# Pacing the MLP evenly over the attention units of a fused top-k attention and MLP kernel

## The chip, the cores and the metric

The kernel runs on one core of one Trainium2 chip. The metric is device time in microseconds (us): 2143.3 us is the median of three runs before the change (2143.25 to 2144.95).

The engines are named as in the profile: PE (TensorE, matrix products; PEld is its weight loads), DVE (VectorE), ACT (ScalarE), POOL (GpSimd), and SP, whose queue issues the DMAs. Each engine works through its own instructions in the order of the program and waits for the others through semaphores.

## The reference

A top-k attention is followed by a two-layer MLP, all in float32. Batch 8, 8 heads, 576 tokens, head size 64; 4608 tokens, model width 512, hidden width 2048.

```
scores = q @ k.T / sqrt(64)
kth    = 32nd largest of each row
scores = where(scores >= kth, scores, -1e9)
attn   = exp(scores - max) / (sum + 1e-9)
x      = (attn @ v), heads side by side      # (4608, 512)
h      = x @ w_in                            # (4608, 2048)
out    = max(0.01 * h, h) @ w_out            # (4608, 512)
```

The weights w_in and w_out arrive as float64. The kernel loads their two 32-bit words and rounds them to float32 itself.

## The kernel before

**Units.** Attention goes in 144 units. A unit is 128 query rows of a pair of heads (two score tiles of 128 x 576), or the 64 rows left over of two pairs of heads. Per batch there are 16 whole units and 2 left-over ones. A unit passes through `scores` (PE products of 64-row operands, then two ACT copies from PSUM to SBUF), `top_k` (four rounds on DVE: MAX8 for both tiles, and in three of them MATCH_REPLACE8, so 14 instructions over 576 elements), `mask` (POOL: for each tile a compare-and-scale into `pen`, and an addition), `exponents` (ACT, with the row sum), `reciprocals` (POOL adds 1e-9, DVE inverts), `normalize` (ACT, one per tile), `transpose_main` (four PE transposes per tile and an ACT copy), `transpose_tail` (two transposes and a copy), and `weigh_values` (PE products with v, ACT copy into the MLP's input x).

**MLP.** Tokens are cut into chunks of mostly 384 (`CHUNKS`, line 51). A chunk's `mlp` is a generator: 16 column blocks f of the hidden layer (4 products `ph` each, then a Prelu on ACT into `gT`), and then per 128 tokens 16 products `pz`, an ACT copy and an output DMA. It yields a cost in columns, so that the caller can issue it in pieces. Both of its PSUM tags together have two buffers.

**Order.** The program's order is written out by hand. Step s of the main loop (lines 340 to 382) handles four units at different ages: top-k of unit s, scores of unit s + 1, mask, exponents, reciprocals and normalize of unit s - 1, and transposes and values of unit s - 2. Five calls of `mlp_steps` lie between these parts, and each adds 1720 cost units to what MLP work may be issued, as long as a chunk is ready. A chunk is ready when the last of its units has passed `weigh_values`.

**Weights.** There are 32 weight chunks of 512 KB. `convert` (twice per step) converts up to two chunks and fetches up to two. `convert_weights` (lines 96 to 113) takes DVE, POOL, ACT, DVE and POOL in turn for one chunk: two integer operations on DVE (lines 104 and 105), a clamp on POOL, two ACT conversions, two more DVE operations (lines 109 and 111) and POOL's product (line 113).

**Loads.** SP's queue issues all loads and stores in program order. q, k and v of a pair of heads are 0.29 MB each, and six of each may be held (`LOADED`). At the start six pairs' q, k and v and two weight chunks are issued before any conversion.

Of the kernel before, what the change touches and what calls it, by code (L numbers as in the profile page):

```python
# [18 lines left out]
def kernel(  # L19
# [28 lines left out]
    KMAX = KLEN[-1]  # L48
    LEFT = S % P
    assert D == 64 and S == 576 and HP == 4 and B % 2 == 0 and LEFT == 64  # L50
    CHUNKS = [256] + [384] * 10 + [256, 128, 128]
    assert sum(CHUNKS) == B * S
    CHMAX = max(CHUNKS)
    LOADED = 6
# [1 line left out]
    const = ctx.enter_context(tc.tile_pool(name="const", bufs=1))  # L56
    xpool = ctx.enter_context(tc.tile_pool(name="xpool", bufs=2))
    loads = ctx.enter_context(tc.tile_pool(name="loads", bufs=LOADED))
    raws = ctx.enter_context(tc.tile_pool(name="raws", bufs=2))
    work = ctx.enter_context(tc.tile_pool(name="work", bufs=2))  # L60
    small = ctx.enter_context(tc.tile_pool(name="small", bufs=4))
    ps_sc = ctx.enter_context(tc.tile_pool(name="ps_sc", bufs=1, space=bass.MemoryType.PSUM))
    ps_tr = ctx.enter_context(tc.tile_pool(name="ps_tr", bufs=2, space=bass.MemoryType.PSUM))
    ps_ml = ctx.enter_context(tc.tile_pool(name="ps_ml", bufs=2, space=bass.MemoryType.PSUM))
# [31 lines left out]
    def convert_weights(dst, raw):  # L96

        lo, hi = raw[:, :, 0], raw[:, :, 1]  # L100
        ex = raws.tile([P, WCH], U32, name="ex")
        man = raws.tile([P, WCH], U32, name="man")
        frac = raws.tile([P, WCH], F32, name="frac")
        nc.vector.tensor_scalar(ex, hi, 20, 0x7FF, ALU.logical_shift_right, ALU.bitwise_and)
        nc.vector.tensor_scalar(man, hi, 0xFFFFF, None, ALU.bitwise_and)
        nc.gpsimd.tensor_scalar(ex, ex, 1151.0, 896.0, ALU.min, ALU.max)  # L106
        nc.scalar.activation(frac, lo, AF.Copy, bias=1.0, scale=2.0 ** -52)
        nc.scalar.activation(ex, ex, AF.Copy, bias=-896.0 * 2.0 ** 23, scale=2.0 ** 23)  # L108
        nc.vector.scalar_tensor_tensor(out=frac, in0=man, scalar=2.0 ** -20, in1=frac,
                                       op0=ALU.mult, op1=ALU.add)  # L110
        nc.vector.scalar_tensor_tensor(out=ex, in0=hi, scalar=0x80000000, in1=ex,  # L111
                                       op0=ALU.bitwise_and, op1=ALU.bitwise_or)
        nc.gpsimd.tensor_tensor(dst, frac, ex.bitcast(F32), ALU.mult)
# [42 lines left out]
    def scores(u):  # L156
        ps = [ps_sc.tile([P, 2, 512], F32, name=f"psc{i}") for i in range(2)]
        for n in range(0, len(u.parts), 2):
            for half in range(2):
                for i, pi, side, r0 in u.parts[n:n + 2]:  # L160
                    qt, kt = qk_of[pi]
                    d = slice(side * D, (side + 1) * D)
                    nc.tensor.matmul(  # L163
                        ps[i][r0:r0 + u.rows, half, 0:HS],
                        qt[d, u.q0:u.q0 + u.rows],
                        kt[d, half * HS:(half + 1) * HS],
                        start=True, stop=True,
                    )
        u.s = []
        for i in range(2):  # L170
            s_sb = work.tile([P, S], F32, name=f"s_sb{i}", bufs=4)
            nc.scalar.copy(s_sb.rearrange("p (h n) -> p h n", h=2), ps[i][:, :, 0:HS])  # L172
            u.s.append(s_sb)

# [12 lines left out]
                src = rest  # L187
            yield

    def mask(u):  # L190
        u.nbias = small.tile([P, 2], F32, name="nbias")
        u.z = small.tile([P, 2], F32, name="z")
        nc.gpsimd.tensor_scalar(u.nbias, u.tops[:, :, 0, 0], -SCALE, None, ALU.mult)
        for i in range(2):
            pen = work.tile([P, S], F32, name="pen")
            nc.gpsimd.tensor_scalar(pen, u.s[i], u.tops[:, i, ROUNDS - 1, 7:8], MASKED,  # L196
                                    ALU.is_lt, ALU.mult)
            nc.gpsimd.tensor_tensor(u.s[i], u.s[i], pen, ALU.add)  # L198

    def exponents(u, i):  # L200
        nc.scalar.activation(u.s[i], u.s[i], AF.Exp, bias=u.nbias[:, i:i + 1], scale=SCALE,  # L201
                             accum_out=u.z[:, i:i + 1])

    def reciprocals(u):
        ze = small.tile([P, 2], F32, name="ze")
        u.rz = small.tile([P, 2], F32, name="rz")
        nc.gpsimd.tensor_scalar(ze, u.z, 1e-9, None, ALU.add)  # L207
        nc.vector.reciprocal(u.rz, ze)  # L208

    def normalize(u, i):  # L210
        nc.scalar.activation(u.s[i], u.s[i], AF.Copy, bias=0.0, scale=u.rz[:, i:i + 1])  # L211
# [48 lines left out]
    def mlp(ch):  # L260

        n = CHUNKS[ch]
        t0 = sum(CHUNKS[:ch])
        x = x_of[ch]
        for f in range(NFC):
            ph = ps_ml.tile([P, 512], F32, name="ph", tag="ml")
            for c in range(HP):
                nc.tensor.matmul(  # L268
                    ph[:, 0:n], w_in[c][:, f * P:(f + 1) * P], x[c][:, 0:n],
                    start=(c == 0), stop=(c == HP - 1),  # L270
                )
            nc.scalar.activation(gT[f][:, 0:n], ph[:, 0:n], AF.Prelu, alpha=SLOPE)  # L272
            yield 4 * max(n, 225)
        for i in range(n // P):
            pz = ps_ml.tile([P, 512], F32, name="pz", tag="ml")
            for f in range(NFC):
                nc.tensor.matmul(  # L277
                    pz[:, 0:DMODEL], gT[f][:, i * P:(i + 1) * P], w_out[f // 4][:, f % 4, :],
                    start=(f == 0), stop=(f == NFC - 1),
                )  # L280
                if f % 4 == 3 and f + 1 < NFC:
                    yield 4 * DMODEL
            o_sb = work.tile([P, DMODEL], F32, name="o_sb")
            nc.scalar.copy(o_sb, pz[:, 0:DMODEL])
            nc.sync.dma_start(out[t0 + i * P:t0 + (i + 1) * P, :], o_sb)
            yield 4 * DMODEL

    ready, owed, running = [], [0.0], [None]
    BUDGET = 1720

    def mlp_steps(budget=BUDGET):
        owed[0] += budget
        while owed[0] > 0:
            if running[0] is None:
                if not ready:
                    owed[0] = 0.0
                    return
                running[0] = mlp(ready.pop(0))
            cost = next(running[0], None)
            if cost is None:  # L300
                running[0] = None
            else:
                owed[0] -= cost

    def unit(n):
        return units[n] if 0 <= n < len(units) else None

    done_tokens = [0] * len(CHUNKS)  # L310

    def attended(u):
        ch, _ = x_at(u.b * S + u.q0)
        done_tokens[ch] += u.rows * len(u.pairs)
        if done_tokens[ch] == CHUNKS[ch] * HP:
            ready.append(ch)

    chunks, raw_chunks = weight_chunks(), []

    def fetch_weights():  # L320
        chunk = next(chunks, None)
        got = load_weights(*chunk) if chunk else None
        if got:
            raw_chunks.append(got)

    with tc.manual_schedule():
        last = {p: n for n, u in enumerate(units) for p in u.pairs}
        load_qk(0)
        scores(units[0])
        for _ in range(2):  # L330
            fetch_weights()

        def load_more(s):

            for of, load, lag in ((qk_of, load_qk, -1), (v_of, load_v, 2)):
                while len(of) < NPAIR and (len(of) < LOADED or last[len(of) - LOADED] + lag <= s):
                    load(len(of))

        load_more(-1)
        for s in range(len(units) + 3):  # L340
            cur, new, old, older = unit(s), unit(s + 1), unit(s - 1), unit(s - 2)
            picks = top_k(cur) if cur else iter(())

            def convert():
                for _ in range(2):
                    if raw_chunks:
                        convert_weights(*raw_chunks.pop(0))
                    fetch_weights()

            if old:  # L350
                mask(old)
            next(picks, None)
            if new:
                scores(new)
            convert()
            mlp_steps()
            next(picks, None)
            if older:
                transpose_main(older, 0)
            mlp_steps()  # L360
            if older:
                transpose_main(older, 1)
            convert()
            mlp_steps()
            next(picks, None)
            if older:
                transpose_tail(older)
            if old:
                exponents(old, 0)
            mlp_steps()  # L370
            if old:
                exponents(old, 1)
                reciprocals(old)
            if older:
                weigh_values(older)
                attended(older)
            mlp_steps()
            next(picks, None)
            if old:
                normalize(old, 0)  # L380
                normalize(old, 1)
            load_more(s)
        mlp_steps(1e9)


# [43 lines left out]
```

## Time and profile before

| what | value |
|---|---|
| median of three runs | 2143.3 us (2143.25 to 2144.95) |
| the profiled execution | 2140.65 us |
| its span, first to last instruction | 2138.9 us |
| mean granted TensorE clock | 0.920 |
| PE busy | 1743.4 us (82%) |
| DVE busy | 1496.2 us (70%) |
| POOL busy | 1174.4 us (55%) |
| ACT busy | 975.9 us (46%) |

Busy times are shares of the span. A stretch (window) of the trace gives the same figures for a part of the span, with the granted clock as a fraction of full speed. A timeline lists instructions in order of time, with equal neighbours merged. A line of the waits says which engine's instruction stood idle for which engine's result, with the sum, the number and the longest.

### The profile page before, as it was taken

The numbers are of one execution on the slowest core, as the hardware profiler recorded it, in microseconds if no ns is written. First come the engines' busy times: TensorE is split into PE (matmuls) and PEld (weight loads), VectorE is DVE, ScalarE is ACT, GpSimd is POOL, SyncE is SP. The second block draws the span as 40 slices with busy tenths as digits, with TensorE's granted clock in tenths as the row PEclk, the third lists the DMA queues.
The fourth block names the chain that finished last, engine by engine and source line by source line (L and its number), as shares of the span: only waits on it lengthen the run. The fifth ranks groups of instructions, "written<-read, shape, count | busy, mean of one in ns | idle before, by whom it ended". The sixth has DMA issues, their size and how long they took to land.

```text
span 2138.9 us, 25069 instructions
## 1 busy us (share of the span) xinstructions
PE 1743.4 (82%) x8864; PEld 1065.6 (50%) x8864; DVE 1496.2 (70%) x3152; ACT 975.9 (46%) x2069; POOL 1174.4 (55%) x934
## 2 busy tenths in 40 slices
PE   1122796897897898898898898798798799699898
PEld 1111554554554554554554554554554555454665
DVE  4788859758857857857857856956955955955760
ACT  1333545435435534535544544544544543543442
POOL 3666547546646645645645645745744844744551
PEclk9999997998898899898799799799799699799999
DMA  4222001000100001000100001000100001000000
GB/s 158 79 79 86 13 10 60 8 9 18 40 22 11 0 6 59 19 6 11 46 21 16 1 6 55 23 1 15 45 17 21 1 1 38 12 1 15 1 10 11
DMA packets 22973, 56.20 MB, mean 26 GB/s; under 512 B 2240, under 2 KB 2240, under 8 KB 22848
## 3 DMA queue, kind: packets, MB, share of 16 engines
q1 hardware_dynamic: 22848, 54.60, 7.5%
q8 instruction: 70, 1.15, 0.2%
q14 instruction: 55, 0.45, 0.1%
HBM read 45.15 MB, written 9.44 MB: 26 GB/s over the span
## 4 chain that ended last, share of the span: by engine, by line
PE 59%; DVE 27%; POOL 7%; ACT 4%; issue 1%; DMA 1%; SPq 0%; POOLq 0%; ACTq 0%; DVEq 0%
PE ph L268 23%; PE pz L277 23%; DVE tops L182 14%; DVE rest L185 12%; PE psc L163 4%; PE main L218 4%; PE po L248 4%; POOL pen L196 3%; POOL s_sb L198 2%; ACT s_sb L201 1%; DVE ex L111 1%; POOL ex L106 1%; ACT ex L108 1%; DMA raw<-in_moe_w_in_dram 1%; PE tail L225 1%
## 5 line engine op out<-in xcount | busy, mean ns | idle before, releaser
L196 POOL TENSOR_SCALAR pen<-s_sb,tops 128x576 f32<-128x576 f32 x288 | 641.3, 2227 | 109.3 <-DVE tops L182 108.7
L182 DVE MAX8 tops<-rest 128x8 f32<-128x576 f32 x864 | 607.9, 745 | 0.0
L268 PE MATMUL ph<-x,w_in 128*128 128x384 f32 (+2 forms) x1792 | 543.7, 451 | 7.5 <-ACT x L258 7.5
L277 PE MATMUL pz<-w_out,gT 128*128 128x512 f32 x1152 | 524.6, 599 | 0.0
L185 DVE MATCH_REPLACE8 rest<-tops,rest 128x576 f32<-128x576 f32 x576 | 423.3, 743 | 0.0
L198 POOL TENSOR_TENSOR s_sb<-s_sb,pen 128x576 f32<-128x576 f32 x288 | 405.8, 1409 | 24.0
L207 POOL TENSOR_SCALAR ze<-z 128x2 f32<-128x2 f32 x144 | 32.4, 225 | 692.1 <-ACT s_sb L201 687.6
L208 DVE RECIPROCAL rz<-ze 128x2 f32<-128x2 f32 x144 | 23.1, 160 | 548.3 <-POOL ze L207 548.3
L268 PEld LDWEIGHTS ph<-x,w_in 128*128 128x128 f32 x1792 | 312.4, 193 | 174.6 <-issue 25.2
L218 PE MATMUL main<-ident,s_sb 128*115 128x128 f32 x1152 | 218.6, 334 | 213.5 <-ACT s_sb L211 213.5
L218 PEld LDWEIGHTS main<-ident,s_sb 128*115 128x115 f32 x1152 | 190.8, 224 | 304.4 <-ACT s_sb L211 226.3
L277 PEld LDWEIGHTS pz<-w_out,gT 128*128 128x128 f32 x1152 | 207.6, 190 | 227.8 <-issue 227.2
L201 ACT ACTIVATE s_sb<-s_sb,nbias 128x576 f32<-128x576 f32 x288 | 222.8, 777 | 207.8 <-POOL s_sb L198 207.8
L248 PE MATMUL po<-wT,vt 115*64 115x128 f32 (+3 forms) x3200 | 250.1, 320 | 43.9 <-ACT wT L226 36.7
L248 PEld LDWEIGHTS po<-wT,vt 115*64 115x64 f32 (+1 forms) x3200 | 208.0, 173 | 104.9 <-ACT wT L226 39.1
L272 ACT ACTIVATE gT<-ph 128x384 f32<-128x384 f32 (+2 forms) x224 | 99.8, 445 | 332.7 <-PE ph L268 332.7
L163 PE MATMUL psc<-kt,qt 64*128 64x288 f32 (+1 forms) x1280 | 222.7, 474 | 34.4 <-ACT s_sb L172 27.0
L211 ACT ACTIVATE s_sb<-s_sb,rz 128x576 f32<-128x576 f32 x288 | 207.2, 768 | 53.6 <-DVE rz L208 53.6
L172 ACT COPY s_sb<-psc 128x576 f32<-128x576 f32 x288 | 167.7, 633 | 108.9 <-PE psc L163 108.9
L185 DVE MATCH_REPLACE8 rest<-tops,s_sb 128x576 f32<-128x576 f32 x288 | 211.7, 743 | 0.0
L220 ACT COPY wT<-main 115x512 f32<-115x512 f32 x288 | 163.1, 590 | 99.6 <-PE main L218 99.0
L182 DVE MAX8 tops<-s_sb 128x8 f32<-128x576 f32 x288 | 201.9, 743 | 7.5 <-ACT s_sb L172 7.5
(26 smaller groups left out, 703.4 us busy)
## 6 DMA issues: line engine op xcount, KB each, us to landing
vt<-in_vk_dram SPq DMA_DIRECT2D x32, 290.0 KB
qt<-in_qT_dram SPq DMA_DIRECT2D x32, 288.0 KB
kt<-in_kT_dram SPq DMA_DIRECT2D x32, 288.0 KB
out_dram<-o_sb SPq DMA_DIRECT2D x36, 256.0 KB
raw<-in_moe_w_in_dram SPq DMA_DIRECT2D x16, 512.0 KB
raw<-in_moe_w_out_dram SPq DMA_DIRECT2D x16, 512.0 KB
```

The source lines that it names most:

```text
L163: nc.tensor.matmul(ps[i][r0:r0 + u.rows, half, 0:HS], qt[d, u.q0:u.q0 + u.rows], kt[d, half * HS:(half + 1) * HS], start=True, stop=True,)
L172: nc.scalar.copy(s_sb.rearrange("p (h n) -> p h n", h=2), ps[i][:, :, 0:HS])
L182: nc.vector.max(out=u.tops[:, i, r, :], in_=src[i])
L185: nc.vector.match_replace(out=rest[i], in_to_replace=u.tops[:, i, r, :], in_values=src[i], imm_value=LOWEST)
L196: nc.gpsimd.tensor_scalar(pen, u.s[i], u.tops[:, i, ROUNDS - 1, 7:8], MASKED, ALU.is_lt, ALU.mult)
L198: nc.gpsimd.tensor_tensor(u.s[i], u.s[i], pen, ALU.add)
L201: nc.scalar.activation(u.s[i], u.s[i], AF.Exp, bias=u.nbias[:, i:i + 1], scale=SCALE, accum_out=u.z[:, i:i + 1])
L211: nc.scalar.activation(u.s[i], u.s[i], AF.Copy, bias=0.0, scale=u.rz[:, i:i + 1])
L218: nc.tensor.transpose(main[0:KLEN[c], c, :], u.s[i][:, c * KSTEP:c * KSTEP + KLEN[c]], ident)
L248: nc.tensor.matmul(po[side * D:(side + 1) * D, o, :], vt[0:KLEN[c], c, side, :], u.wT[0:KLEN[c], i, c, r0:r0 + n], start=(c == 0), stop=(c ...
L268: nc.tensor.matmul(ph[:, 0:n], w_in[c][:, f * P:(f + 1) * P], x[c][:, 0:n], start=(c == 0), stop=(c == HP - 1),)
L277: nc.tensor.matmul(pz[:, 0:DMODEL], gT[f][:, i * P:(i + 1) * P], w_out[f // 4][:, f % 4, :], start=(f == 0), stop=(f == NFC - 1),)
```

## The change

- `CHUNKS` begins with 128 and 256 tokens and ends with 256 and 128.
- `mlp` yields twice as often: in the middle of a `ph` block, and after every second `pz` product. `mlp_steps` takes its budget as an argument. `slot_budget` divides the MLP work that is ready and not yet issued by the number of slots (six per step) up to and with the step at which the next chunk gets ready.
- The softmax chain is one step longer. Mask stays with unit s - 1, but its two tiles are issued apart; exponents and reciprocals are now with unit s - 2, and normalize, transposes and values with unit s - 3 (`LAG = 3`). A chunk becomes ready at the end of the step of its last unit. `s_sb` has five buffers for four, `small` five for four, `pen` one for two. The addition of 1e-9 is a function of its own (`sums`).
- A weight conversion has two stages. The first ends after the ACT conversions; the rest is issued by the next call of `convert`. `convert` now handles one chunk and is called three times in odd steps and four times in even ones. `raw` has three buffers for two, and `frac` lies in the raw tile itself.
- At the start four pairs' q and k alternate with four weight chunks on SP's queue, and four v loads follow. Further loads start at step 4.

```diff
-    CHUNKS = [256] + [384] * 10 + [256, 128, 128]
+    CHUNKS = [128, 256] + [384] * 10 + [256, 128]
...
+        frac = lo.bitcast(F32)
+        ex = raws.tile([P, WCH], U32, name="ex", bufs=2)
+        man = raws.tile([P, WCH], U32, name="man", bufs=2)
...
         nc.scalar.activation(ex, ex, AF.Copy, bias=-896.0 * 2.0 ** 23, scale=2.0 ** 23)
+        yield
         nc.vector.scalar_tensor_tensor(out=frac, in0=man, scalar=2.0 ** -20, in1=frac,
...
+    def mask(u, i):
+        if i == 0:
+            u.nbias = small.tile([P, 2], F32, name="nbias")
+            u.z = small.tile([P, 2], F32, name="z")
+            nc.gpsimd.tensor_scalar(u.nbias, u.tops[:, :, 0, 0], -SCALE, None, ALU.mult)
+        pen = work.tile([P, S], F32, name="pen", bufs=1)
...
+    def sums(u):
+        u.ze = small.tile([P, 2], F32, name="ze")
+        nc.gpsimd.tensor_scalar(u.ze, u.z, 1e-9, None, ALU.add)
...
+                if c == 1:
+                    yield 2 * max(n, 225)
...
-                if f % 4 == 3 and f + 1 < NFC:
-                    yield 4 * DMODEL
+                if f % 2 and f + 1 < NFC:
+                    yield 2 * DMODEL
...
+    def mlp_cost(ch):
+        n = CHUNKS[ch]
+        return NFC * HP * max(n, 225) + n // P * NFC * DMODEL
...
+    for n, u in enumerate(units):
         ch, _ = x_at(u.b * S + u.q0)
         done_tokens[ch] += u.rows * len(u.pairs)
         if done_tokens[ch] == CHUNKS[ch] * HP:
+            ready_at.append((n + LAG, ch))
...
+    def slot_budget(s):
+        after = [at for at, _ in ready_at if at >= s]
+        return backlog[0] / ((after[0] + 1 - s if after else 1) * SLOTS)
...
+    def finish_conversions():
+        while converting:
+            next(converting.pop(0), None)
+    def convert():
+        finish_conversions()
+        if raw_chunks:
+            converting.append(convert_weights(*raw_chunks.pop(0)))
+            next(converting[0])
+        fetch_weights()
...
         scores(units[0])
+        fetch_weights()
+        for p in range(1, HP):
+            load_qk(p)
+            fetch_weights()
+        for p in range(HP):
+            load_v(p)
...
+            budget = slot_budget(s)
+            next(picks, None)
+            if old:
+                mask(old, 0)
+            if new:
+                scores(new)
+            convert()
+            mlp_steps(budget)
+            if older:
+                exponents(older, 0)
+            if oldest:
+                normalize(oldest, 0)
+            if older:
+                exponents(older, 1)
+                sums(older)
+            if old:
+                mask(old, 1)
+            mlp_steps(budget)
+            next(picks, None)
+            convert()
+            if oldest:
+                transpose_main(oldest, 0)
+                normalize(oldest, 1)
+            mlp_steps(budget)
+            if oldest:
+                transpose_main(oldest, 1)
+            next(picks, None)
+            convert()
+            mlp_steps(budget)
+            if older:
+                reciprocals(older)
+            if oldest:
+                transpose_tail(oldest)
+            next(picks, None)
+            if s % 2 == 0:
+                convert()
+            mlp_steps(budget)
+            if oldest:
+                weigh_values(oldest)
+            mlp_steps(budget)
+            attended(s)
+            if s >= HP:
+                load_more(s)
```

## Rows read from the trace of the kernel before

**Rows 1.** The page: busy time of each engine, and the chain's shares.

```profile
PE 1743.4 (82%) x8864; PEld 1065.6 (50%) x8864; DVE 1496.2 (70%) x3152; ACT 975.9 (46%) x2069; POOL 1174.4 (55%) x934
...
PE 59%; DVE 27%; POOL 7%; ACT 4%; issue 1%; DMA 1%; SPq 0%; POOLq 0%; ACTq 0%; DVEq 0%
```

**Rows 2.** Windows: stretch, length, busy per engine (instructions), clock, DMA share, GB/s.

```profile
0.00:45.61 45.61, 10.23 (x32) 5.99 (x32) 20.27 (x36) 10.13 (x16) 9.00 (x15) 1.00 0.54 186
46.00:228.00 182.00, 45.49 (x229) 30.60 (x230) 149.20 (x260) 68.28 (x133) 112.40 (x99) 1.00 0.23 75
390.00:495.00 105.00, 102.68 (x431) 56.24 (x428) 62.78 (x137) 41.32 (x89) 49.03 (x38) 1.00 0.02 6
495.00:555.00 60.00, 39.85 (x260) 29.41 (x259) 55.27 (x121) 36.55 (x77) 44.29 (x35) 0.73 0.11 35
2106.83:2138.90 32.07, 28.29 (x162) 20.29 (x160) 0.00 (x0) 5.29 (x18) 0.00 (x0) 1.00 0.02 9
```

**Rows 3.** Timeline of DVE (start, duration, instruction): reciprocals of two units in succession.

```profile
509.79 0.15 DVE L208 RECIPROCAL rz<-ze 128x2 f32<-128x2 f32 x1
...
519.49 0.15 DVE L208 RECIPROCAL rz<-ze 128x2 f32<-128x2 f32 x1
```

**Rows 4.** Timeline of PE through most of a step in a PE-bound stretch.

```profile
434.28 1.24 PE L163 MATMUL psc<-kt,qt 64*128 64x288 f32 x8
435.45 2.85 PE L268 MATMUL ph<-x,w_in 128*128 128x384 f32 x8
438.13 0.60 PE L218 MATMUL main<-ident,s_sb 128*115 128x128 f32 x4
438.57 2.75 PE L268 MATMUL ph<-x,w_in 128*128 128x384 f32 x8
441.15 0.60 PE L218 MATMUL main<-ident,s_sb 128*115 128x128 f32 x4
...
444.17 0.38 PE L225 MATMUL tail<-ident,s_sb 128*116 128x128 f32 x2
444.39 3.60 PE L277 MATMUL pz<-w_out,gT 128*128 128x512 f32 x8
447.92 1.31 PE L248 MATMUL po<-wT,vt 115*64 115x128 f32 x20
```

**Rows 5.** Timeline of PE: the last chunk of 128 tokens.

```profile
2106.83 14.56 PE L268 MATMUL ph<-x,w_in 128*128 128x128 f32 x128
2121.22 13.90 PE L277 MATMUL pz<-w_out,gT 128*128 128x512 f32 x32
```

**Rows 6.** Groups of ACT: busy us, mean ns of one, idle before and its releaser.

```profile
L201 ACT ACTIVATE s_sb<-s_sb,nbias 128x576 f32<-128x576 f32 x288 | 222.8, 777 | 207.8 <-POOL s_sb L198 207.8
L211 ACT ACTIVATE s_sb<-s_sb,rz 128x576 f32<-128x576 f32 x288 | 207.2, 768 | 53.6 <-DVE rz L208 53.6
L172 ACT COPY s_sb<-psc 128x576 f32<-128x576 f32 x288 | 167.7, 633 | 108.9 <-PE psc L163 108.9
L220 ACT COPY wT<-main 115x512 f32<-115x512 f32 x288 | 163.1, 590 | 99.6 <-PE main L218 99.0
L272 ACT ACTIVATE gT<-ph 128x384 f32<-128x384 f32 x160 | 78.6, 491 | 281.2 <-PE ph L268 281.2
```

**Rows 7.** Waits: who waited for whom, us in total, times, longest.

```profile
PE main L218 <- ACT s_sb L211: 213.5, 70, 27.2
...
DVE ex L111 <- ACT ex L108: 30.3, 31, 3.8
```

**Rows 8.** Groups of DVE: the two integer operations of a weight conversion.

```profile
L105 DVE TENSOR_SCALAR man<-raw 128x512 uint32<-128x512 uint32 x32 | 30.5, 953 | 0.0
...
L104 DVE TENSOR_SCALAR ex<-raw 128x512 uint32<-128x512 uint32 x32 | 15.8, 494 | 14.3 <-DMA raw<-in_moe_w_in_dram 14.3
```

**Rows 9.** Timeline of DVE in a conversion that follows another.

```profile
133.76 1.49 DVE L105 TENSOR_SCALAR man<-raw 128x512 uint32<-128x512 uint32 x1
```

More of the change, by code (lines that the diff above doesn't have):

```diff
@@ L58 @@
     loads = ctx.enter_context(tc.tile_pool(name="loads", bufs=LOADED))
-    raws = ctx.enter_context(tc.tile_pool(name="raws", bufs=2))
+    raws = ctx.enter_context(tc.tile_pool(name="raws", bufs=3))
     work = ctx.enter_context(tc.tile_pool(name="work", bufs=2))
-    small = ctx.enter_context(tc.tile_pool(name="small", bufs=4))
+    small = ctx.enter_context(tc.tile_pool(name="small", bufs=5))
     ps_sc = ctx.enter_context(tc.tile_pool(name="ps_sc", bufs=1, space=bass.MemoryType.PSUM))
@@ L100, in convert_weights @@
         lo, hi = raw[:, :, 0], raw[:, :, 1]
-        ex = raws.tile([P, WCH], U32, name="ex")
-        man = raws.tile([P, WCH], U32, name="man")
-        frac = raws.tile([P, WCH], F32, name="frac")
+        frac = lo.bitcast(F32)
+        ex = raws.tile([P, WCH], U32, name="ex", bufs=2)
+        man = raws.tile([P, WCH], U32, name="man", bufs=2)
         nc.vector.tensor_scalar(ex, hi, 20, 0x7FF, ALU.logical_shift_right, ALU.bitwise_and)
@@ L170, in scores @@
         for i in range(2):
-            s_sb = work.tile([P, S], F32, name=f"s_sb{i}", bufs=4)
+            s_sb = work.tile([P, S], F32, name=f"s_sb{i}", bufs=5)
             nc.scalar.copy(s_sb.rearrange("p (h n) -> p h n", h=2), ps[i][:, :, 0:HS])
@@ L188, in top_k @@
             yield
[L190 to L198, printed above, removed]
+    def mask(u, i):
[4 more added lines that the diff above has]
+        pen = work.tile([P, S], F32, name="pen", bufs=1)
+        nc.gpsimd.tensor_scalar(pen, u.s[i], u.tops[:, i, ROUNDS - 1, 7:8], MASKED,
+                                ALU.is_lt, ALU.mult)
+        nc.gpsimd.tensor_tensor(u.s[i], u.s[i], pen, ALU.add)
     def exponents(u, i):
@@ L202, in exponents @@
                              accum_out=u.z[:, i:i + 1])
+    def sums(u):
+        u.ze = small.tile([P, 2], F32, name="ze")
+        nc.gpsimd.tensor_scalar(u.ze, u.z, 1e-9, None, ALU.add)
     def reciprocals(u):
-        ze = small.tile([P, 2], F32, name="ze")
         u.rz = small.tile([P, 2], F32, name="rz")
-        nc.gpsimd.tensor_scalar(ze, u.z, 1e-9, None, ALU.add)
-        nc.vector.reciprocal(u.rz, ze)
+        nc.vector.reciprocal(u.rz, u.ze)
     def normalize(u, i):
@@ L271, in mlp @@
                 )
+                if c == 1:
+                    yield 2 * max(n, 225)
             nc.scalar.activation(gT[f][:, 0:n], ph[:, 0:n], AF.Prelu, alpha=SLOPE)
-            yield 4 * max(n, 225)
+            yield 2 * max(n, 225)
         for i in range(n // P):
@@ L285, in mlp, with mlp_steps @@
             nc.sync.dma_start(out[t0 + i * P:t0 + (i + 1) * P, :], o_sb)
[L286 to L291, printed above, removed]
+            yield 2 * DMODEL
+    def mlp_cost(ch):
+        n = CHUNKS[ch]
+        return NFC * HP * max(n, 225) + n // P * NFC * DMODEL
+    ready, running = [], [None]
+    backlog, owed = [0.0], [0.0]
+    def mlp_steps(budget):
         owed[0] += budget
@@ L303, in mlp_steps @@
                 owed[0] -= cost
+                backlog[0] -= cost
+    LAG = 3
     def unit(n):
         return units[n] if 0 <= n < len(units) else None
-    done_tokens = [0] * len(CHUNKS)
-    def attended(u):
+    done_tokens, ready_at = [0] * len(CHUNKS), []
+    for n, u in enumerate(units):
         ch, _ = x_at(u.b * S + u.q0)
@@ L315, in attended @@
         if done_tokens[ch] == CHUNKS[ch] * HP:
-            ready.append(ch)
+            ready_at.append((n + LAG, ch))
+    assert [ch for _, ch in ready_at] == list(range(len(CHUNKS)))
+    def attended(s):
+        for at, ch in ready_at:
+            if at == s:
+                ready.append(ch)
+                backlog[0] += mlp_cost(ch)
+    def slot_budget(s):
+        after = [at for at, _ in ready_at if at >= s]
+        return backlog[0] / ((after[0] + 1 - s if after else 1) * SLOTS)
+    SLOTS = 6
+    converting = []
     chunks, raw_chunks = weight_chunks(), []
@@ L329 @@
         scores(units[0])
-        for _ in range(2):
+        fetch_weights()
+        for p in range(1, HP):
+            load_qk(p)
             fetch_weights()
+        for p in range(HP):
+            load_v(p)
         def load_more(s):
-            for of, load, lag in ((qk_of, load_qk, -1), (v_of, load_v, 2)):
+            for of, load, lag in ((qk_of, load_qk, -1), (v_of, load_v, LAG)):
                 while len(of) < NPAIR and (len(of) < LOADED or last[len(of) - LOADED] + lag <= s):
                     load(len(of))
-        load_more(-1)
-        for s in range(len(units) + 3):
-            cur, new, old, older = unit(s), unit(s + 1), unit(s - 1), unit(s - 2)
+        for s in range(len(units) + LAG):
+            cur, new, old = unit(s), unit(s + 1), unit(s - 1)
+            older, oldest = unit(s - 2), unit(s - LAG)
             picks = top_k(cur) if cur else iter(())
[L344 to L348, printed above, removed]
+            budget = slot_budget(s)
+            next(picks, None)
             if old:
-                mask(old)
-            next(picks, None)
+                mask(old, 0)
             if new:
@@ L355 @@
             convert()
-            mlp_steps()
-            next(picks, None)
-            if older:
[L359 to L364, printed above, removed]
-            next(picks, None)
[L366 to L382, printed above, removed]
+            mlp_steps(budget)
[9 more added lines that the diff above has]
+            mlp_steps(budget)
+            next(picks, None)
+            convert()
[8 more added lines that the diff above has]
+            mlp_steps(budget)
+            if older:
+                reciprocals(older)
+            if oldest:
+                transpose_tail(oldest)
+            next(picks, None)
+            if s % 2 == 0:
[7 more added lines that the diff above has]
+                load_more(s)
+        finish_conversions()
         mlp_steps(1e9)
```

## The prediction

> **What bounds the kernel now.** I read the page's busy shares and the chain of waits first. PE is busy 82% of the span and DVE 70%, and the chain that ended last is PE for 59% and DVE for 27% [rows 1]: no single engine bounds it, so it must be two in turn. The windows show that. From 390 to 495 us PE is busy 102.7 of 105 us at granted clock 1.00 while DVE works 62.8; from 495 to 555 DVE is busy 55.3 of 60 while PE has 39.9 at a mean clock of 0.73 [rows 2]. The two stretches are one round of 12 units, one 384-token chunk. The old budget gives 5 × 1720 = 8600 cost units per unit of attention, and a chunk costs 16·4·384 + 3·16·512 = 49,152, so its MLP is done in 5.7 units (PE-bound, 105 us) and the other 6.3 run at DVE's pace, 9.70 us from one reciprocal to the next [rows 3], 61 us. A round is 165 us, 13.75 us per unit. Ahead of the rounds lies a start in which PE does little: 0 to 46 us, with DVE busy 20 us, then seven steps of 26.0 us (46 to 228) that convert four weight chunks each [rows 2].
>
> **The change, part by part.** The sum is made against the profiled execution: span 2138.9 us, 2140.65 us in all, so 1.75 lie around the span. The median of the runs shown is 2.65 us higher; that is added at the end.
>
> *PE's own work per unit, full clock* [rows 4]. Scores 1.17 us (434.28 to 435.45), two groups of main transposes 0.44 each (438.13 to 438.57), tail 0.22, value product 1.3: 3.57. The 16 left-over units of 144 have up to twice the score and value work: 0.25 on average. MLP: one f of a 384 chunk is 2.58 us (438.57 to 441.15), 16 make 41.3; one 128-row output group is 13.8 (32 instructions in 13.9 [rows 5]), three make 41.4; 82.7 per chunk, 6.89 per unit. Together 10.7 us. The check: one chunk's 82.7 plus 5.7 units × 3.57 is 103, and the PE-bound stretch holds 102.7 [rows 2].
>
> *Even pacing.* With MLP spread over 12 units, each step has 10.7 us of PE and 9.75 of DVE (9.70 [rows 3] plus the waits around the reciprocal). Neither is idle half the round any more, so the floor is PE's 10.7.
>
> *The new order within a step, which I think decides.* In before, `normalize(old)` is the last thing in a step, so PE's transposes wait for it in the DVE-bound stretch only (213.5 us in 70 waits [rows 7]). In after, ACT's in-order queue has in each step: two score copies of the new unit, exp, normalize 0, exp, copy of main 0, normalize 1. The copies wait for PE's scores at the step's start, and normalize 1 must end before PE's main 1. From the start of the scores that is 1.24 (scores) + 2 × 0.633 + 0.777 + 0.768 + 0.777 + 0.590 + 0.768 [rows 4, 6] = 6.2, plus a Prelu of 0.49 for each f that ends in slots 1 and 2 (0.9 of them in the ph half of a chunk, none in the pz half: 0.2 on average), so 6.4. PE's own work up to that point is 1.17 + 3 slots × 1.15 + 0.44 = 5.06. PE stands about 1.3 us per step, in front of main 0 and main 1. After main 1 three slots, tail and value product follow, whose copies are done in time. So 12.0 us per unit. Bounds: 10.7 if ACT gets ahead, and 12.9 if two Prelus stand in the chain and every hand-over costs 0.1 (6.2 + 1.0 + 0.1 − 5.06 = 2.2).
>
> *The other waits added.* `sums` on POOL waits for ACT's second exp; the second mask pair stands behind it, but its exp comes a whole step later. DVE's reciprocal, now ahead of the last pick round, waits for `sums`; that round (1.4 us) and the next unit's picks stand behind it. At 12.0 us a step DVE has 2.2 us to spare, so I cost it at nothing; without the slack it would be up to 1.4 per step. `pen` in one buffer is written and read by POOL alone, in order: nothing. Half-size MLP yields add no instruction: nothing. The extra `s_sb`, `small` and `raw` buffers only remove waits.
>
> *The start.* The same 32 conversions remain. DVE is busy 149.2 us in seven steps of four [rows 2], so (149.2 − 7 × 9.75) / 28 = 2.9 us each. What two stages remove is DVE's in-line wait for ACT's exponent (30.3 us in 31 waits, up to 3.8 [rows 7]), since a round of picks now lies between. On SP, 8 score loads and 3 raw chunks, then 4 value loads, replace 12 score and 6 value loads ahead of the third raw chunk; raw 4 waits for the first conversion's second stage with the value loads behind it, which nobody needs before step 3. DVE's 25 idle us at the start [rows 2] should halve to 13. At 4, 3, 4, 3... conversions a step, 32 are done at the end of step 8: 9 × 9.75 + 32 × 2.9 + 13 + 6 for hand-overs with POOL = 200 us. Before, step 8 ends at 228 + 9.7 = 238. Gain 38, bounds 15 and 50.
>
> *A rule against this.* The second integer operation of a conversion took 1.49 us beside POOL's product [rows 9]; it is 0.95 on average and the first 0.49, with one shape [rows 8]. The Trainium skill, "SBUF — State Buffer" (Who interferes with whom), says that DVE in a two-port mode and GpSimd hold their shared ports for a whole instruction; that row agrees. By that rule, and with conversions now meeting POOL's mask between picks, each might wait a whole pen operation. The sum by it would be some 40 us later, an estimate from POOL's mean of 2.2 us. My sum keeps 2.9 per conversion, which already holds such waits.
>
> *Steps 9 to 26* run the 128 and 256 chunks at 3.5 and 4.6 us of MLP a step. DVE needs 9.75; the ACT chain gives 6.4 + 0.44 + three short slots 2.2 + 0.22 + 1.3 = 10.5. I take 11.0, as the clock may dip where PE is 75% busy (0.73 at 66% [rows 2]); bounds 10 and 12. 18 × 11.0 = 198.
>
> *Steps 27 to 134*: nine 384 chunks, 108 units × 12.0 = 1296 (1156 to 1393).
>
> *Steps 135 to 142*: the tenth chunk in 8 steps, 82.7 + 8 × 3.8 = 113; slots are long enough to cover the ACT chain. *Steps 143 to 146*: the 256 chunk, 16 × 1.73 + 2 × 13.8 = 55, and four units' transposes and values, 10: 65. (One f at 256 is two thirds of 2.58.) *Last*: the 128 chunk alone, 32.07 us as before [rows 2, 5].
>
> Sum: 200 + 198 + 1296 + 113 + 65 + 32 = 1904, with 1.75 around it 1906, and 2.65 to the median: 1908.
>
> **Rivals.** *A, PE back to back*: ACT's chain hides, 10.7 a unit, 108 × 1.3 = 140 less: 1768. For it: PE was busy 98% of a stretch with all of attention in it [rows 2]. Against: there no normalize stood behind the same step's score copies.
>
> *B, longer chain*: both Prelus in it, 12.9 a unit (+97), and longer steps at the start: 2005 to 2045. For it: ACT has some twelve short instructions a step and each hand-over is in series. Against: their mean durations already hold the queueing in before.
>
> *C, the clock, slower than before*: PE's new gaps in every step bring the granted clock down all through steps 27 to 134, and PE's work stretches. In the DVE-bound stretch PE had gaps in every unit and the clock was 0.73 [rows 2]; at that, 10.7 / 0.73 = 14.7 a unit, 108 × 2.7 = 291 more: about 2200. It decides below 0.75, where a unit costs 14.2 and the sum meets 2143. Against: that stretch had a third of the work per unit, and where PE was 98% busy the clock was 1.00; I expect 89%.
>
> **How the numbers follow.** Forecast (a unit of 11.5 to 12.5: 1850 to 1965) 0.55; A and what lies toward it 0.18; B 0.22; C 0.05. The likeliest time is 1908. The range leaves out C, the upper end of B and the lowest end of A: 1775 to 2020. Faster by over 0.2% (what the runs can tell from no change) 0.95, within 0.2% 0.01, slower 0.04.
>
> **What would show it.** Windows of 12 units anywhere from 500 to 1700 us should be alike: PE about 89% busy, DVE about 80%, clock 0.97 or more, and 144 us long. The waits should show PE's main transposes on ACT's normalize about 1.3 us per unit, in two pieces, and reciprocals 12.0 us apart. DVE's waits for ACT's exponent in the conversions should be gone and step 8 end near 200 us. I am wrong if the reciprocals stand 10.7 apart (A), if ACT's waits per unit exceed 2 us (B), or if the clock of those windows is below 0.9 (C).

## The result and the profile after

The changed kernel takes 1967.5 us, the median of four runs (1965.1 to 1969.7). Against the kernel before, timed beside it, the ratio is 0.918, with a 95% interval of 0.916 to 0.919: 176 us faster. The forecast was 1908, the range 1775 to 2020. The profiled execution has a span of 1967.9 us.

The page's busy times and its chain's shares, as in [rows 1]:

```profile
PE 1651.5 (84%) x8864; PEld 963.6 (49%) x8864; DVE 1498.1 (76%) x3152; ACT 987.9 (50%) x2069; POOL 1189.6 (60%) x934
...
PE 71%; ACT 18%; POOL 4%; issue 3%; DVE 2%; DMA 0%; SPq 0%; POOLq 0%; ACTq 0%
```

DVE has gone from the chain (27% to 2%), and ACT has come in (4% to 18%) although its own work is the same. So PE and DVE no longer take turns, and a wait between PE and ACT is the new bound.

Windows of the changed kernel (stretch, length, busy PE, PEld, DVE, ACT, POOL, then clock, DMA share, GB/s): up to step 1, the start from step 1 to step 8, the even part from step 27 to 134, and the end from where PE begins the 256-token chunk.

```profile
0.00:26.92 26.92, 7.41 (x24) 4.28 (x24) 18.32 (x34) 7.67 (x12) 7.89 (x13) 1.00 0.61 203
26.92:210.22 183.30, 52.96 (x285) 40.53 (x285) 156.09 (x280) 70.53 (x140) 129.57 (x104) 0.75 0.28 91
408.00:1748.00 1340.00, 1213.64 (x6452) 680.86 (x6452) 1057.91 (x2268) 710.40 (x1479) 833.40 (x648) 0.99 0.06 21
1871.00:1967.90 96.90, 93.16 (x472) 64.44 (x470) 2.18 (x6) 29.49 (x72) 11.78 (x10) 1.00 0.03 11
```

The even part is 108 units in 1340 us, 12.4 us a unit, with PE busy 91%, DVE 79%, and the clock at 0.99. In [rows 2] PE and DVE were each over 90% busy in turn, and the clock was 0.73 in one of the two stretches. Two reciprocals of this part, in DVE's timeline, stand 12.18 us apart; in [rows 3] it was 9.70 in a DVE-bound stretch:

```profile
539.32 0.17 DVE L211 RECIPROCAL rz<-ze 128x2 f32<-128x2 f32 x1 [2.38 <-POOL ze L207]
...
551.50 0.17 DVE L211 RECIPROCAL rz<-ze 128x2 f32<-128x2 f32 x1 [2.39 <-POOL ze L207]
```

DVE now stands in front of the reciprocal for 2.4 us a step: that is slack, and the bound is elsewhere. The timeline of PE and ACT through most of a step shows where:

```profile
522.10 1.24 PE L164 MATMUL psc<-kt,qt 64*128 64x288 f32 x8
...
523.27 3.70 PE L282 MATMUL pz<-w_out,gT 128*128 128x512 f32 x8
...
523.43 1.18 ACT L173 COPY s_sb<-psc 128x576 f32<-128x576 f32 x2 [0.94 <-PE psc L164]
...
524.50 0.79 ACT L202 ACTIVATE s_sb<-s_sb,nbias 128x576 f32<-128x576 f32 x1
...
525.27 0.77 ACT L214 ACTIVATE s_sb<-s_sb,rz 128x576 f32<-128x576 f32 x1
...
525.93 0.77 ACT L202 ACTIVATE s_sb<-s_sb,nbias 128x576 f32<-128x576 f32 x1
...
526.81 0.60 PE L221 MATMUL main<-ident,s_sb 128*115 128x128 f32 x4
...
527.45 0.59 ACT L223 COPY wT<-main 115x512 f32<-115x512 f32 x1 [0.66 <-PE main L221]
...
527.93 0.78 ACT L214 ACTIVATE s_sb<-s_sb,rz 128x576 f32<-128x576 f32 x1
...
528.76 0.69 PE L221 MATMUL main<-ident,s_sb 128*115 128x128 f32 x4 [1.35 <-ACT s_sb L214]
```

Read it as one line of hand-overs: scores end, ACT copies them, exp, normalize 0, exp, PE's main 0, ACT's copy of it, normalize 1, PE's main 1, which PE waits for 1.35 us. From the scores' start to main 1 it is 6.66 us. The waits say the same, in the whole execution and then in the even part alone (408 to 1748 us):

```profile
PE main L221 <- ACT s_sb L214: 271.7, 169, 31.5
...
PE main L221 <- ACT s_sb L214: 125.3, 124, 1.4
```

In [rows 7] that wait was 213.5 us in 70 waits, in stretches that DVE bounded anyway; now it is in every step of the even part, 1.16 us per unit, and PE is the engine that matters.

In the start, the first MAX8 of step 1 comes at 26.92 us and that of step 9 at 210.22 (DVE's timeline):

```profile
26.92 1.41 DVE L183 MAX8 tops<-s_sb 128x8 f32<-128x576 f32 x2
...
210.22 1.41 DVE L183 MAX8 tops<-s_sb 128x8 f32<-128x576 f32 x2
```

In the kernel before the same two lines of DVE's timeline are

```profile
46.01 1.40 DVE L182 MAX8 tops<-s_sb 128x8 f32<-128x576 f32 x2
...
237.80 1.41 DVE L182 MAX8 tops<-s_sb 128x8 f32<-128x576 f32 x2
```

The start gains 27.6 us up to step 9, and 19.1 of them are there when step 1 begins. The other 8.5 come in steps 1 to 8, which take 183.3 us where they took 191.8: steps of some 24 us with four conversions and of 21.6 with three, in place of seven steps of 26.0 with four and one of 9.7 with none. So the order of the loads gives most of the gain, by these rows; it was not tried alone.

### The profile page after: what moved, and what is told of

The parts are those of the page before. It is cut to its first block, busy times and chain, and to the rows that moved or that the text cites. A ratio compares the mean times of both kernels' runs of the same rounds, so it can differ in the third digit from the quotient of the medians.

```text
span 1967.9 us, 25462 instructions
## 1 busy us (share of the span) xinstructions
PE 1651.5 (84%) x8864; PEld 963.6 (49%) x8864; DVE 1498.1 (76%) x3152; ACT 987.9 (50%) x2069; POOL 1189.6 (60%) x934
## 4 chain that ended last, share of the span: by engine, by line
PE 71%; ACT 18%; POOL 4%; issue 3%; DVE 2%; DMA 0%; SPq 0%; POOLq 0%; ACTq 0%
PE pz L282 25%; PE ph L271 18%; PE psc L164 9%; PE po L251 9%; PE main L221 8%; ACT s_sb L214 7%; ACT s_sb L202 4%; ACT wT L223 4%; PE tail L228 2%; ACT s_sb L173 2%; ACT gT L277 1%; POOL pen L197 1%; POOL w_in L114 1%; POOL ex L106 1%; POOL w_out L114 1%
## 5 line engine op out<-in xcount | busy, mean ns | idle before, releaser
L271 PE MATMUL ph<-x,w_in 128*128 128x384 f32 (+2 forms) x1792 | 575.4, 457 | 0.0
L282 PE MATMUL pz<-w_out,gT 128*128 128x512 f32 x1152 | 542.0, 603 | 0.0
L221 PE MATMUL main<-ident,s_sb 128*115 128x128 f32 x1152 | 203.0, 301 | 273.0 <-ACT s_sb L214 271.7
L199 POOL TENSOR_TENSOR s_sb<-s_sb,pen 128x576 f32<-128x576 f32 x288 | 411.9, 1430 | 24.0
L221 PEld LDWEIGHTS main<-ident,s_sb 128*115 128x115 f32 x1152 | 156.9, 187 | 399.8 <-ACT s_sb L214 336.0
L164 PE MATMUL psc<-kt,qt 64*128 64x288 f32 (+1 forms) x1280 | 203.0, 439 | 38.6 <-ACT s_sb L173 31.2
L214 ACT ACTIVATE s_sb<-s_sb,rz 128x576 f32<-128x576 f32 x288 | 222.9, 774 | 0.0
L251 PEld LDWEIGHTS po<-wT,vt 115*64 115x64 f32 (+1 forms) x3200 | 162.0, 140 | 88.4 <-issue 82.6
L251 PE MATMUL po<-wT,vt 115*64 115x128 f32 (+3 forms) x3200 | 195.9, 272 | 1.0 <-ACT wT L223 1.0
L164 PEld LDWEIGHTS psc<-kt,qt 64*128 64x128 f32 (+1 forms) x1280 | 110.4, 182 | 108.2 <-issue 45.5
```

Of the source, the lines that this page charges most:

```text
L164: nc.tensor.matmul(ps[i][r0:r0 + u.rows, half, 0:HS], qt[d, u.q0:u.q0 + u.rows], kt[d, half * HS:(half + 1) * HS], start=True, stop=True,)
L221: nc.tensor.transpose(main[0:KLEN[c], c, :], u.s[i][:, c * KSTEP:c * KSTEP + KLEN[c]], ident)
L251: nc.tensor.matmul(po[side * D:(side + 1) * D, o, :], vt[0:KLEN[c], c, side, :], u.wT[0:KLEN[c], i, c, r0:r0 + n], start=(c == 0), stop=(c ...
L271: nc.tensor.matmul(ph[:, 0:n], w_in[c][:, f * P:(f + 1) * P], x[c][:, 0:n], start=(c == 0), stop=(c == HP - 1),)
L282: nc.tensor.matmul(pz[:, 0:DMODEL], gT[f][:, i * P:(i + 1) * P], w_out[f // 4][:, f % 4, :], start=(f == 0), stop=(f == NFC - 1),)
```

## Experiments

All times are medians of four runs beside the kernel before (2143.6 to 2144.6 us in these comparisons). A unit's cost is the distance of the reciprocals of steps 26 and 122 divided by 96: 12.39 us in the changed kernel.

### E1: both normalize operations at the head of the step

```diff
                 mask(old, 0)
+            if oldest:
+                normalize(oldest, 0)
+                normalize(oldest, 1)
             if new:
                 scores(new)
...
-            if oldest:
-                normalize(oldest, 0)
...
-                normalize(oldest, 1)
```

> The changed kernel with one edit: both normalize operations of a unit are issued at the head of the step, ahead of the score copies, so that nothing on ACT's queue that waits for the same step's scores stands in front of them. Theory (ACT's queue): the time above PE's own 10.7 us per unit is the serial stretch scores, copies, exp, normalize 0, exp, copy of main 0, normalize 1, main 1; without it a unit costs 10.8 to 11.1 us instead of 12.4, PE's waits of the main transposes on normalize fall from 272 us to under 60, and the time is 1790 to 1830 us. Rival (the clock or PE itself: PE's 90% busy is all that its waits for PSUM and weight loads allow): a unit stays above 12 us and the time is 1940 to 1967. Rival (DVE and POOL take over, since the sums wait for the second exp): 11.6 us or more, 1870 to 1910.

Measured: 1756.0 us, ratio to before 0.819 (0.818 to 0.821); a unit costs 10.66 us. A window of the even part:

```profile
515.00:661.00 146.00, 146.00 (x797) 86.11 (x795) 132.32 (x285) 86.44 (x185) 105.24 (x83) 1.00 0.07 23
```

PE is busy all 146.0 us at full clock, and over the whole execution the wait of the main transposes on normalize is small:

```profile
PE main L221 <- ACT s_sb L214: 26.8, 4, 23.3
```

It is the theory's case; it even goes below its lowest time, since steps 10 to 26 fell to 9.70 us a step as well (the wait had bound those too). Both rivals are out. This one order costs the change 211 us.

### E2: the kernel before with even pacing alone

```diff
-    BUDGET = 1720
-    def mlp_steps(budget=BUDGET):
+    def mlp_steps(budget):
...
+    LAG, SLOTS = 2, 5
+    def slot_budget(s):
+        after = [at for at, _ in ready_at if at >= s]
+        return backlog[0] / ((after[0] + 1 - s if after else 1) * SLOTS)
```

(with the half-size yields, `ready_at`, `mlp_cost` and `backlog` of the change)

> The kernel before with the even pacing and the finer MLP pieces alone; softmax chain, weight conversion, chunks and loads stay as they were. Theory (the gain is the pacing, and the longer chain costs more than it gives): in the old order normalize stands at the end of the step, behind no score copy of the step in which its transposes run, so a unit costs 10.8 to 11.3 us, and with the old start (step 8 ending at 238 us) the time is 1800 to 1850 us, below the changed kernel's 1967. Rival (the longer chain is what lets the pacing work, since mask, exp and reciprocal of one unit must all fit in one step): 12.5 us or more per unit, 1990 to 2060 us.

Measured: 1796.9 us, ratio 0.838 (0.837 to 0.840); a unit costs 10.87 us; step 8's reciprocal is at 236.9 us, as before (236.4). The same window:

```profile
515.00:661.00 146.00, 146.00 (x775) 85.11 (x775) 134.09 (x288) 89.40 (x187) 105.11 (x82) 1.00 0.03 11
```

The theory holds: pacing alone, with the finer pieces that it needs, takes 347 us off, twice the whole change. The rival, that the longer chain makes pacing possible, is out.

### E3: the changed kernel with the old pacing

```diff
-            budget = slot_budget(s)
+            budget = 8600 / SLOTS
```

> The changed kernel with the old budget: 8600 cost units per step, 1433 in each of the six slots, and all the rest of the change kept. Theory (pacing is the whole gain of the middle): rounds of 12 units with a PE-bound part of 5.7 units at 18 us and the rest at about 10.2 us, 165 to 170 us a round instead of 149, so 150 to 210 us more than the changed kernel: 2115 to 2180 us. Rival (the longer chain or the buffers carry much of the gain): under 2060 us.

Measured: 2243.8 us, ratio 1.047 (1.045 to 1.049): slower than before, and past the theory's range. A round of 12 units takes 172 to 180 us (163 to 165 before).

```profile
515.00:661.00 146.00, 119.23 (x577) 73.02 (x576) 102.79 (x221) 66.09 (x138) 80.02 (x62) 0.84 0.09 30
```

So all else in the change, without the pacing, costs 100 us, although its start is some 28 us shorter. In the sparse part of a round steps are mostly 10.5 to 12 us apart where before had 9.70: the PE-ACT stretch binds there even with little MLP in it. The granted clock may have a part in this: it is 0.68 in a sparse part from 1080 to 1140 us (0.73 in such a part of the kernel before [rows 2], which DVE bounds), and the four main transposes of a tile take 1.20 us there, against 0.60 in the step shown above. How the 100 us divide between the order and the clock was not tried.

### E4: one-stage conversion

```diff
             next(converting[0])
+            finish_conversions()
         fetch_weights()
```

> The changed kernel with the conversion in one piece again: each call finishes the chunk that it begins. Theory (the two stages take away DVE's in-line waits for ACT's exponent, in part): each of 32 conversions waits 1 to 2 us more, and the start takes 15 to 45 us longer, with nothing changed after step 9: 1980 to 2010 us. Rival (what the start gains comes from the loads and buffers alone, as POOL's mask still stands in the way of the second stage): within 8 us of 1967.

Measured: 1972.1 us, ratio 0.919 (0.916 to 0.922), the same as the changed kernel's 0.918. DVE's wait for ACT's exponent, in E4 and in the changed kernel, is

```profile
DVE ex L112 <- ACT ex L108: 36.8, 30, 2.9
...
DVE ex L112 <- ACT ex L108: 24.0, 11, 4.2
```

(30.3 us in 31 waits before [rows 7]). Two stages take 12.8 us off this wait, in fewer and longer pieces, but DVE's second integer operation of a conversion gets slower. Its groups, again in E4 and in the changed kernel:

```profile
L105 DVE TENSOR_SCALAR man<-raw 128x512 uint32<-128x512 uint32 x32 | 13.5, 421 | 0.0
...
L105 DVE TENSOR_SCALAR man<-raw 128x512 uint32<-128x512 uint32 x32 | 33.2, 1037 | 0.0
```

That is 19.7 us more: with two stages 17 of the 32 start beside POOL's product and take about 1.5 us, with one stage none does. Step 9 begins at 213.6 us in E4 and at 210.2 in the changed kernel. The rival's time holds. Its reason was POOL's mask; these rows show POOL's product besides, which takes back what the waits give.

### E5: normalize 1 right behind normalize 0

```diff
                 normalize(oldest, 0)
+                normalize(oldest, 1)
...
                 transpose_main(oldest, 0)
-                normalize(oldest, 1)
```

> The changed kernel with one edit: normalize 1 is issued right behind normalize 0, still behind the score copies and the first exp, instead of behind the copy of main 0. It grades the serial sum. Theory (the time above 10.7 us is that stretch, operation by operation): the second exp and the copy of main 0 leave the chain to main 1, so what is left is main 0's wait of about 0.6 us and the Prelus; a unit costs 11.2 to 11.6 us, and with 108 units in the even part and some gain before them the time is 1860 to 1900 us, in the middle between 1967 and the 1756 of the version with both ahead of the copies. Rival (only standing behind the score copies matters): no more than 20 us below 1967. Rival (only main 1's wait matters): about 1760 to 1790.

Measured: 1811.2 us, ratio 0.845 (0.844 to 0.846); a unit costs 11.11 us. Better than forecast, a little below the theory's unit and well below its time, as steps 9 to 26 gained too (step 26's reciprocal at 390 against 408 us). Of the 1.73 us a unit that E1 takes away, normalize 1's place behind the second exp, main 0 and main 0's copy costs 1.28, and both standing behind the score copies and the first exp 0.45.

### E6: E1 with the old chunks

```diff
-    CHUNKS = [128, 256] + [384] * 10 + [256, 128]
+    CHUNKS = [256] + [384] * 10 + [256, 128, 128]
```

> The version with both normalize operations ahead of the score copies (1756 us), with the chunks of the kernel before: 256 first, and 256, 128, 128 last. Theory (the smaller first chunk lets PE begin four steps earlier, in steps that DVE bounds anyway): PE has four steps less for its MLP outside the PE-bound part, 15 to 35 us more, 1770 to 1790. Rival (the chunk sizes don't matter, since the same MLP work must be done by the end and PE is idle at the start either way): within 8 us of 1756.

Measured: 1777.3 us, ratio 0.829 (0.828 to 0.830), 21 us more than E1: as the theory says. A 128-token chunk first instead of last is worth 21 us when PE is the bound.

### E7: E1 with the second mask pair later

```diff
-                sums(older)
-            if old:
-                mask(old, 1)
             mlp_steps(budget)
             next(picks, None)
             convert()
+            if older:
+                sums(older)
+            if old:
+                mask(old, 1)
```

> The version with both normalize operations ahead of the score copies (1756 us), and the sums and the second mask pair issued behind the second conversion of a step instead of ahead of it. Theory (what DVE still waits for in the start is POOL's clamp, queued behind the sums, which wait for ACT's second exp, and behind 3.6 us of mask): the waits of up to 3.9 us in one conversion per step go, 20 to 25 us off the start, and step 8's reciprocal comes at 180 to 187 us instead of 205; 1728 to 1738 us. Rival (the waits move to the next conversion, as POOL has the same work): within 8 us of 1756.

Measured: 1736.1 us, ratio 0.810 (0.808 to 0.811), 20 us less than E1. Step 8's reciprocal is at 183.81 us, and the wait has gone:

```profile
DVE ex L112 <- ACT ex L108: 3.4, 9, 1.2
```

So what was left of DVE's wait was POOL's order: the clamp stood behind `sums`, which waits for ACT's second exp, and behind a mask pair. The two were moved together, so their shares are not known.

### E8: E7 with three conversions in every step

```diff
             next(picks, None)
-            if s % 2 == 0:
-                convert()
             mlp_steps(budget)
```

> The version of e7 with three conversions in every step instead of four and three. Theory (DVE's conversion work is the same and only its waits count): steps of the start get 1 to 2 us shorter on average but go on two steps longer, so within 8 us of e7. Rival (the fourth conversion, squeezed in at the end of even steps, is what costs: its second integer operation stands beside POOL's product): 8 to 20 us below e7.

Measured: 1728.2 us, ratio 0.806 (0.805 to 0.807), 7.9 us less than E7, on the line between the two. Step 26's reciprocal comes at 354.6 against 363.3 us, so the whole difference is made in the start; which operation of the fourth conversion costs it was not tried. This is the fastest version here: by the two ratios to the kernel before, 0.878 of the changed kernel's time (0.875 to 0.881 from the ends of their intervals).

### E9: the changed kernel with the shorter chain

```diff
-    LAG = 3
+    LAG = 2
...
+            if old:
+                mask(old, 0)
+                mask(old, 1)
...
+            if old:
+                exponents(old, 0)
+            mlp_steps(budget)
+            if old:
+                exponents(old, 1)
+                sums(old)
+                reciprocals(old)
...
+            if old:
+                normalize(old, 0)
+                normalize(old, 1)
             mlp_steps(budget)
```

(transposes and values of unit s - 2 in the places of the kernel before)

> The changed kernel (pacing, chunks, two-stage conversion, loads) with the softmax chain of the kernel before: mask, exp, reciprocal and normalize of a unit in one step, transposes and values in the next. What the longer chain is worth by itself, against the 1756 us of the version that keeps it and has both normalize operations first. Theory (the longer chain is not needed once normalize stands ahead of the next step's score copies): a unit costs 10.7 to 10.9 us as with the pacing alone (10.87), the start is that of the changed kernel or a little longer, as both mask pairs stand ahead of the conversions on POOL, and the time is 1755 to 1785. Rival (the long chain gives DVE and ACT slack that is needed): 1800 or more.

Measured: 1794.0 us, ratio 0.837 (0.836 to 0.838), between theory and rival. A unit costs 10.83 us, as the theory says. The rest is in the start: the reciprocal of unit 24 (step 25 here, step 26 in E1) comes at 405.4 us against E1's 384.2. From 26 to 240 us DVE stands in front of the reciprocal, a wait that E1 does not have in this stretch:

```profile
DVE rz L211 <- POOL ze L207: 36.8, 8, 4.6
```

So in the start the longer chain does give the slack that the rival speaks of, and in the even part it is not needed. What the two mask pairs ahead of the conversions' clamps on POOL have to do with this wait was not tried. Against E1 the longer chain is worth 38 us: (10.83 − 10.66) × 108 = 18 in the units, and about 20 in the start. And E9 is only 3 us below E2, which has the old chain with the old loads, chunks and conversion.

## Why the prediction was right, and where it was off

**The bound and the floor.** Right. PE's own 10.7 us per unit, summed from [rows 4, 5], is what E1 measures: 10.66 with PE busy all the time. That the pacing lets DVE and PE overlap is E2: 347 us.

**The new order decides.** Right, and the wait named is the one that binds: PE's main transposes on normalize, in front of main 1 above all. What the stretch costs was put too small. The forecast was 1.3 us above PE's own work; measured is 12.41 − 10.7 = 1.7 over steps 27 to 134, which is 44 us over 108 units. Of the 1.7, PE's idle time is 1.16 (125.3 us in 108 units), near the forecast; PE's recorded busy time is 11.24 a unit (1213.64 / 108) where the sum has 10.7. What makes it longer was not traced; the rows show a clock of 0.99, and 0.69 us for the main group behind a wait where the one before it takes 0.60.

The term that failed is the stretch to main 1, 6.4 us with a Prelu in half the cases. By PE's timeline it is 6.73 us on average over the 108 steps, and the rest of the step 5.70, where the sum has 10.7 − 5.06 = 5.64. In the step shown two pz pieces (3.5 us) precede main 0, so main 0 and its copy lie on the chain (ACT waits 0.66 us for main 0), and it is 6.66 us with no Prelu. I had taken ACT's queue alone as the chain and PE's part beside it. In 72 of the 108 steps PE comes to main 0 without a wait, so there main 0 starts no sooner than PE's own work allows. By E5 the part from normalize 0 to normalize 1 is the larger piece, 1.28 of 1.73; it holds the second exp as well as the pass through PE, and the two were not tried apart.

**The start.** The forecast put step 8's end at 200 us; DVE begins step 9 at 210.2. The term that failed is the 6 us for hand-overs with POOL: from step 1 to step 9 DVE is idle 183.30 − 156.09 = 27.2 us, nearly all of it in the wait for the exponent (24.0 us in the whole execution), which I had called gone. E7 shows why and takes the wait away. The idle at the first loads came out better than put: 8.6 us (26.92 less the 18.32 that DVE is busy), where the sum has 13.

**The rest.** Steps 9 to 26 came out at 11.1 us (11.0 forecast), steps 135 to 142 at 113 us (113). The end is as put, 97 us, from where PE begins the 256-token chunk (1870.7 us); but DVE begins step 143 at 1863.0, and the sum, which goes over from DVE's steps to PE's work there, has nothing for the 8 us between. The profiled span of 1967.9 us is 64 above the 1904 of the sum: 44 in the units, 10 in the start, 8 at this seam, 2 in steps 9 to 26.

**Rivals.** A (PE back to back) was not this kernel, but it is E1. B described the right thing at too high a price: ACT's waits stayed below its sign of 2 us per unit. Still, the time of 1967.5 lies 2 us above the 1850 to 1965 that had the largest chance, though the unit's 12.41 us lies inside its 11.5 to 12.5. C did not occur: the clock was 0.99 in the even part, with a wait in every step, the longest 1.4 us. The rule on ports: the conversions took some 2.8 us of DVE each, (156.09 − 8 × 9.75) / 28, about as summed, so nothing came on top of the sum. But 0.6 us of each is such a wait, by E4 (1037 against 421 ns in one operation); what POOL paid is below.

**What I did not see.** I took the longer chain as given and asked only what it costs. E2 shows that the pacing alone would have given twice the gain, and E3 that the rest by itself loses 100 us. The longer chain gains its 38 us only with normalize ahead of the copies (E1 against E9); with the order of the change it loses, as E9 is 173 us faster than the changed kernel.

## What to carry to other kernels

When work is paced evenly, a chain of hand-overs inside a step can come onto the path, as here, so check, for each in-order queue, which instruction of this step stands ahead of one that is ready from the last. Issue first what is ready (here normalize), then what waits for another engine (the score copies). And sum a cross-engine chain through every engine that it visits, not along one queue: the piece from normalize 0 to normalize 1, which passes through PE and back, was the dearest.

## What the runs showed of the hardware

One mask addition of POOL took 3.05 us in the start, and another 1.41, near the usual (POOL's timeline of the changed kernel; the mean of all 288 is 1.43):

```profile
38.99 3.05 POOL L199 TENSOR_TENSOR s_sb<-s_sb,pen 128x576 f32<-128x576 f32 x1
...
50.33 1.41 POOL L199 TENSOR_TENSOR s_sb<-s_sb,pen 128x576 f32<-128x576 f32 x1
```

Beside the long one DVE ran four conversion operations without a gap, and then went on with its picks:

```profile
38.82 0.68 DVE L110 SCALAR_TENSOR_TENSOR raw<-man,raw 128x512 f32<-128x512 uint32 x1
39.42 0.68 DVE L112 SCALAR_TENSOR_TENSOR ex<-raw,ex 128x512 uint32<-128x512 uint32 x1
40.02 0.42 DVE L104 TENSOR_SCALAR ex<-raw 128x512 uint32<-128x512 uint32 x1
40.36 0.42 DVE L105 TENSOR_SCALAR man<-raw 128x512 uint32<-128x512 uint32 x1
40.69 1.41 DVE L183 MAX8 tops<-rest 128x8 f32<-128x576 f32 x2
```

POOL's instruction ends at 42.04, 1.35 us after DVE's MAX8 begins at 40.69. That is about its usual duration, as if it had stood still until the four were through. The Trainium skill, "SBUF — State Buffer" (Who interferes with whom), says that DVE operations with two SBUF inputs or in a two-port mode and GpSimd's shut each other out; these rows agree, and here POOL is the one that pays. In the other direction DVE pays, where POOL's product starts first (both timelines of the changed kernel):

```profile
45.46 1.40 POOL L114 TENSOR_TENSOR w_in<-raw,ex 128x512 f32<-128x512 f32 x1 [1.47 <-DVE ex L112]
45.63 1.51 DVE L105 TENSOR_SCALAR man<-raw 128x512 uint32<-128x512 uint32 x1
```

The same operation took 0.42 us at 40.36.
